# One mask product per bank and split value products for the last 64 queries of an attention kernel

## The chip, the core and the metric

The kernel runs on one core of one Trainium2 chip. Times are device microseconds of that core for one launch. Five engines run side by side, each through its own instructions in their order: TensorE (PE, with its weight loads listed apart as PEld), VectorE (DVE), ScalarE (ACT), GpSimd (POOL) and SyncE (SP, which issues most DMAs). TensorE writes its products to PSUM, eight banks of 512 float32 columns on 128 partitions.

## The reference

Three layers follow one another: attention, a mixture of experts, and a two-layer network.

```python
scores = (q @ k.transpose(0, 1, 3, 2)) / sqrt(D)      # q, k, v: B, H, S, D = 4, 8, 576, 64
scores = where(triu(ones(S, S), k=1), -1e9, scores)   # causal mask
a = exp(scores - scores.max(-1)); a /= a.sum(-1) + 1e-9
local = a @ v
q_p = where(q > 0, q, exp(q) - 1) + 1
mem_out = (q_p @ M_prev) / (q_p . z_prev + 1e-6)
attn = g * mem_out + (1 - g) * local                  # g = sigmoid(beta), per head
x = moe(attn as 2304 rows of 512)    # 8 experts, the best one for each row that is not skipped
out = leaky_relu(x @ w_in) @ w_out   # 512 -> 2048 -> 512
```

## The kernel before, in words

The 32 pairs of batch and head are worked in eight groups `n` of four heads. The 576 queries of a head lie in blocks of 128, 128, 128, 128 and 64 (`ROWS`). A slot (`slot`, L716) is one head and one half of its queries: half `hf` = 0 holds queries 0 to 255, half 1 queries 256 to 575. There are 32 slots of each half. In a slot

- `mm`/`mx` (L726, L733) make the scores with queries on partitions, and DVE takes each row's maximum; `q2t`/`q2e` (L753, L758) turn minus that maximum into two extra rows of the second operand;
- the second `mm` (L772 to L776) makes the scores again, with keys on partitions, in the banks that `BLK` lists. An entry (o, j, r0) is key block j against the queries from r0 on, written from column o. Half 0 has one bank, half 1 three. Each entry is a product L772 (128 x 128 weights, float32r), a product L774 that adds the low part and the maximum (66 rows), and, where the block touches the diagonal, a product L776 of the triangle `tri16` and `negi` (both bfloat16), which adds -1e30 above the diagonal;
- `exp` (L781, ACT) writes the exponentials of a bank to `pT`;
- `pv` (L802) multiplies them with the values and a column of ones, in float32, 64 queries at a time: 64 columns of `pT` are the weights, 65 columns of `vn` stream through, and the sums land on partitions 0 to 63 (m = 0) or 64 to 127 (m = 64) of a PSUM tile `pv`. Each float32 product is two weight loads and two matmuls in the trace. A query block of 128 has products on both halves of the partitions in turn; the last block, of 64 queries, has its five (one for each key block) all on partitions 0 to 63.

When both heads of a pair are done, `final` (L820) divides by the sums of the ones column (`f1` to `f3`: L834, L835, L839, L844), scales into `xb` (`f4`: L852, L854) and adds the memory part on POOL (`f5`: L862). The tile `pv` is one of two banks (`PVB` = 2), and it is free when `f4` is done. There are 32 finals, 16 of them of half 1, which hold the last query block.

The order on each engine is made by a list scheduler in the program (`Sched`): each task has an engine, a duration in ns, its predecessors, a key (its due time) and what it takes of the pools ("s": six score banks, "v": the two `pv` banks, and so on). In its simulated time the scheduler gives an idle engine the ready task of lowest key. The durations are constants in the code: for `pv` 181 for each key block of a full query block and 122 for each of the last one. Between these tasks the same engines also work on other things that the scheduler puts in: the copies that split q and k into high and low parts, 32 chunks of a weight conversion on ACT, DVE and POOL (L319 to L339), the routing of rows to experts, and at the end the first tiles of the first expert (`early`).

Of the kernel before, what the change touches and what calls it, by code (L numbers as in the profile page):

```python
# [10 lines left out]
F32 = mybir.dt.float32  # L11
# [6 lines left out]
AF = mybir.ActivationFunctionType  # L18
ALU = mybir.AluOpType
# [10 lines left out]
EK, WS = 39944.504, 485.0  # L30
PT0, PTX, PTH, PT2 = 0.3, -0.1, -0.17, -1427.4
MAN = {ET.PE, ET.Activation, ET.DVE, ET.Pool}
BLK = [[[(0, 0, 0), (256, 1, 128)]], [[(0, 0, 0), (320, 3, 128)], [(0, 1, 0), (320, 4, 256)], [(0, 2, 0)]]]
OFF = [[0], [0, 512, 896]]
SP = [[[(0, 0, 0, 128), (1, 128, 0, 256)]], [[(2, 0, 0, 384)], [(3, 0, 0, 512)], [(4, 0, 0, 256)], [(4, 0, 256, 320)]]]
EXPS = [[384], [512, 384, 320]]
# [94 lines left out]
class K:  # L131
# [579 lines left out]
    def slot(self, n, b, g, hf, h, T, d, get, put):  # L711
        nc, add, st = self.nc, self.sc.add, self.st
        O1, O2, O3, O4 = OFS[hf]
        q1, k1, k2, qb, vn, col = d["q1"], d["k1"], d["k2"], d["qb"], d["vn"], d["col"]
        xs = (0,) if hf == 0 else (0, 1, 2)
        ni, i0 = 2 + hf, 2 * hf  # L716
        u = {}
        kd = get(*[("k1", n, h, x) for x in xs], *[("q1", n, h, x) for x in xs[hf:]])
        ttr = []
        for p, parts in enumerate(SP[hf]):  # L720
            def mm(parts=parts, p=p):
                if p == 0:
                    u["m8"] = self.m8.pop(0)
                u["s", p] = s = self.T_tile()
                for i, o, c0, w in parts:
                    nc.tensor.matmul(s[:, o:o + w], col(1, h, 128 * i), k1[:, h, c0:c0 + w], start=True, stop=True)  # L726

            def mx(parts=parts, p=p):
                s = u.pop(("s", p))
                for i, o, c0, w in parts:  # L730
                    R = ROWS[i]
                    m = u["m8"][:R, i - i0:i - i0 + 1]
                    nc.vector.tensor_tensor_reduce(out=self.y[:R, 0:w], in0=s[:R, o:o + w], in1=self.mb[:R, max(0, MB[i] + c0):max(0, MB[i] + c0) + w],  # L733
                                                   scale=1.0, scalar=-3e38 if c0 == 0 else m, op0=ALU.add, op1=ALU.max, accum_out=m)
            pe = sum(max(w / 2.4 + 3, ROWS[i] / 1.2) for i, o, c0, w in parts)
            dv = sum(w / .96 + 73 + (60 if c0 else 0) for i, o, c0, w in parts)
            a = add("PE", pe, mm, kd + (get(("m8r", n)) if 0 else []), T + p, ["s"] + (["m8"] if p == 0 else []))
            put(("s", n), a)
            ttr.append(add("DVE", dv, mx, [a] + ttr[-1:], T + O1 * (p + 1) / len(SP[hf]), (), ["s"]))

        def sp():
            m8 = u["m8"]
            self.m8.append(m8)
            q = qb[:, i0:i0 + ni, h, 64:66]
            nc.vector.tensor_reduce(out=q[:, :, 0], in_=m8[:, 0:ni, None], axis=AX.X, op=ALU.max, negate=True)
            nc.vector.scalar_tensor_tensor(q[:, :, 1], m8[:, 0:ni], -1.0, q[:, :, 0].bitcast(F32), op0=ALU.mult, op1=ALU.subtract)
        put("ttr", *ttr)
        a = add("DVE", 145, sp, ttr, T + O1, (), ["m8"])

        def q2t():  # L750
            u["qt"] = t = self.T_tile(F32R)
            for x in range(ni):
                nc.tensor.transpose(t[:66, 128 * x:128 * x + 128], qb[:, i0 + x, h], self.idr)  # L753

        def q2e():
            w = 256 + 64 * hf
            u["q2"] = q2 = self.ap3.tile([128, 320], F32R, tag="q2", name="q2")
            nc.scalar.activation(q2[:66, :w], u.pop("qt")[:66, :w].bitcast(F32), AF.Copy)  # L758
        a = add("PE", (114, 175)[hf], q2t, [a] + get(*[("ql", n, x) for x in xs[hf:]]), T + O2, ["s"])
        for x in xs[hf:]:  # L760
            put(("q2t", n, x), a)
        a = add("ACT", (264, 318)[hf], q2e, [a], T + O2 + 1, ["q2"], ["s"])
        kd = get(*[("k2", n, h, x) for x in xs])
        ex = {}
        nb = len(BLK[hf])
        for p, (bank, o1, w) in enumerate(zip(BLK[hf], OFF[hf], EXPS[hf])):
            def mm(bank=bank, p=p):
                u["t", p] = t = self.T_tile()
                for o, j, r0 in bank:
                    q0, q1_ = 256 * hf + r0, (256, S)[hf]  # L770
                    R, w = ROWS[j], q1_ - q0
                    nc.tensor.matmul(t[:, o:o + w], col(0, h, 128 * j), q1[:, h, q0:q1_], start=True, stop=False)  # L772
                    diag = q0 == 128 * j
                    nc.tensor.matmul(t[:, o:o + w], col(2, h, 128 * j)[:66], u["q2"][:66, r0:r0 + w], start=False, stop=not diag)  # L774
                    if diag:
                        nc.tensor.matmul(t[:, o:o + R], self.tri16, self.negi[:, :R], start=False, stop=True)  # L776

            def exp(o1=o1, w=w, p=p):
                if p == 0:
                    u["pT"] = self.ap3.tile([128, (384, 1216)[hf]], F32, tag=f"pT{hf}", name="pT", bufs=2)  # L780
                nc.scalar.activation(u["pT"][:, o1:o1 + w], u.pop(("t", p))[:, 0:w], AF.Exp, scale=0.125)  # L781

            pe = sum(2 * max((256 + 64 * hf - r0) / 2.4 + 3, ROWS[j] / 1.2) + 60 * (256 * hf + r0 == 128 * j) for o, j, r0 in bank)
            m_ = add("PE", pe, mm, [a] + kd, T + O3 + p, ["s"])
            put(("st", n), m_)
            e_ = add("ACT", w / 1.2 + 51, exp, [m_] + list(ex.values())[-1:], T + O3 + p + .5,
                     [f"pT{hf}"] if p == 0 else [], ["s"] + (["q2"] if p == nb - 1 else []))
            for o, j, r0 in bank:
                ex[j] = e_
        pos = {j: OFF[hf][k] + o - r0 for k, bank in enumerate(BLK[hf]) for o, j, r0 in bank}  # L790
        r, hh = h // 2, h % 2
        pvs = []
        for x in range(ni):
            def pv(x=x):
                if hh == 0 and x == 0:
                    st["pv", n, hf, r] = self.psP.tile([128, 512], F32, tag="p", name="pv")
                t, i = st["pv", n, hf, r], i0 + x
                R, o = ROWS[i], 130 * x + 65 * hh
                for j in range(i + 1):
                    c = pos[j] + 128 * x  # L800
                    for m in range(0, R, 64):
                        nc.tensor.matmul(t[m:m + 64, o:o + 65], u["pT"][:, c + m:c + m + 64], vn[:, j, h], start=(j == 0), stop=(j == i))  # L802
            i = i0 + x
            first = hh == 0 and x == 0
            pvs.append(add("PE", sum(181 if ROWS[i] == 128 else 122 for j in range(i + 1)), pv,
                           [ex[j] for j in range(i + 1)] + pvs[-1:] + get(("lv", n)) + ([] if first else get(("pv0", n, hf, r))), T + O4 + x,
                           ["v"] if first else [], [f"pT{hf}"] if x == ni - 1 else []))
            if first:
                put(("pv0", n, hf, r), pvs[-1])
        put(("vuse", n), *pvs)  # L810
        if hf:
            put("pvs1", *pvs)
        put(("pv", n, hf, r), *pvs)
        if hh == 1:
            self.final(n, b, g, hf, r, T + O4 + FIN, d["ec"], get, put)

    def final(self, n, b, g, hf, r, T, ec, get, put):
        nc, add, st = self.nc, self.sc.add, self.st
        ni, i0 = 2 + hf, 2 * hf
        u = {}  # L820
        cuts = [(0, 2, 128), (2, 3, 64)][:1 + hf]

        def mem():
            u["s"] = s = self.T_tile()
            for x in range(ni):
                nc.tensor.matmul(s[:, 130 * x:130 * x + 130], ec(r, i0 + x), self.mm[b % 2][:, 2 * g + r], start=True, stop=True)

        def f1():
            u["n"] = self.nl.pop(0)
            pv = st.pop(("pv", n, hf, r))  # L830
            u["sv"] = u["s"][:, 0:130 * ni].rearrange("p (x c) -> p x c", x=ni)
            u["pv"] = pv[:, 0:130 * ni].rearrange("p (x h c) -> p x h c", x=ni, h=2)
            for x0, x1, R in cuts:
                nc.vector.tensor_scalar(u["n"][:R, x0:x1, 1], u["pv"][:R, x0:x1, :, D], 1e-9, None, op0=ALU.add)  # L834
            nc.vector.tensor_scalar(u["n"][:, 0:ni, 0], u["sv"][:, :, 128:130], 1e-6, None, op0=ALU.add)  # L835

        def f2():
# [8 lines left out]
        def f4():  # L846
# [2 lines left out]
                st["xb", b] = self.ap2.tile([128, NB, DM], F32, tag="xb", name="xb")  # L849
            u["m2"] = m2 = self.ap2.tile([128, 3, 2, D], F32, tag="m2", name="m2")  # L850
            for x0, x1, R in cuts:
                nc.vector.tensor_tensor(xv(x0, x1, R), u["pv"][:R, x0:x1, :, 0:D],  # L852
                                        rl[:R, x0:x1, 1, :, None].to_broadcast([R, x1 - x0, 2, D]), op=ALU.mult)
            nc.vector.tensor_tensor(m2[:, 0:ni], u["sv"][:, :, 0:128].rearrange("p x (h d) -> p x h d", h=2),  # L854
                                    rl[:, 0:ni, 0, :, None].to_broadcast([128, ni, 2, D]), op=ALU.mult)
# [6 lines left out]
            nc.gpsimd.tensor_tensor(xv(x0, x1, R), u["m2"][:R, x0:x1], xv(x0, x1, R), op=ALU.add)  # L862
        m = add("PE", 226 * ni, mem, get(("eT", n), ("mm", b)), T - MK, ["s"])
        put(("mem", n), m)
        a = add("DVE", 140 + 70 * hf, f1, [m] + get(("pv", n, hf, r)), T, ["nl"])
        a = add("DVE", (100, 135)[hf], f2, [a], T)
        a = add("DVE", 80, f3, [a] + get("gl"), T, (), ["nl"])
        war = get(("xbuse", b - 2))
# [810 lines left out]
```

## Time and profile before

| | us |
|---|---|
| three runs: lowest, median, highest | 886.28, 889.01, 889.37 |
| the profiled execution | 887.11 |
| its span from first to last instruction | 885.5 |
| TensorE busy in it (share) | 850.9 (96%) |
| VectorE, ScalarE, GpSimd busy (share) | 630.7 (71%), 480.8 (54%), 198.5 (22%) |

Some 1.6 us of the profiled execution lie outside its span. The attention fills the first 325 us or so, the experts run until 490 us, and the rest is the two-layer network. A busy share of TensorE counts matmuls that overlap in its pipeline, and their ends are modelled; how long a piece of its work takes is therefore read from the start of its first matmul to the start of the next piece.

### The profile page before, as it was taken

To read this page: it belongs to the slowest core of one execution; us is meant where nothing else is said; L and a number is where in the kernel's file an instruction comes from. 1 tells how busy PE (TensorE), PEld (TensorE's weight loads), DVE (VectorE), ACT (ScalarE), POOL (GpSimd) and SP (SyncE) were. 2 spreads that over 40 slices of the span, in tenths; PEclk is the share of its full clock that TensorE was granted. 3 is DMA by queue.
4 is the path that set the end of the run, shared out by engine and by line. 5 is a ranking of instruction groups with operands and counts; after the bars stand their busy time and mean duration, and the time that the engine had idled before them with its cause. 6 is when DMAs were issued, how large, how long until landed. Compare 5 with 4: busy or idle time off the path is not lost. (4 is left out here: it accounts for less than half of the span.)

```text
span 885.5 us, 19666 instructions
## 1 busy us (share of the span) xinstructions
PE 850.9 (96%) x7432; PEld 758.6 (86%) x7432; DVE 630.7 (71%) x1786; ACT 480.8 (54%) x921; POOL 198.5 (22%) x262
## 2 busy tenths in 40 slices
PE   6999999999999899998999999999999999999997
PEld 5887888887788777676667899999999999999997
DVE  6779787879878986578575589765656565656565
ACT  8897886877876562666554355433333333333332
POOL 5546444654532733222220000000000000000000
PEclk9699997999999999999999999999999999999999
DMA  6747765566357394899562401010101010101000
GB/s 147 191 130 187 200 198 141 124 152 199 75 193 274 123 336 127 298 341 344 176 244 89 171 1 48 1 49 1 48 1 49 1 48 2 48 2 48 1 24 24
DMA packets 103947, 107.61 MB, mean 122 GB/s; under 512 B 69661, under 2 KB 69789, under 8 KB 103828
## 3 DMA queue, kind: packets, MB, share of 16 engines
q1 hardware_dynamic: 101190, 100.90, 36.7%
q0 software_dynamic: 2640, 5.21, 2.0%
q8 instruction: 67, 1.10, 0.5%
q14 instruction: 50, 0.41, 0.2%
HBM read 81.57 MB, written 25.86 MB: 121 GB/s over the span
## 5 line engine op out<-in xcount | busy, mean ns | idle before, releaser
L1594 PE MATMUL g<-sw,ah 128*128 128x256 f32 x448 | 126.0, 281 | 0.0
L1593 PE MATMUL g<-sw,ah 128*128 128x256 f32 x448 | 125.7, 281 | 0.0
L1545 DVE SCALAR_TENSOR_TENSOR ua<-ua 128x512 f32<-128x512 f32 x72 | 49.6, 689 | 80.2 <-ACT ua L1494 80.2
L1494 ACT ACTIVATE ah<-ua 128x384 fp32r<-128x384 f32 (+1 forms) x72 | 38.8, 539 | 110.4 <-PE g L1595 78.4
L1494 ACT ACTIVATE ua<-t 128x512 f32<-128x512 f32 x72 | 43.0, 597 | 101.1 <-PE t L1538 101.1
L733 DVE CUSTOM_DVE_ANT_0 v<-t,v 128x512 f32<-128x512 f32 (+4 forms) x160 | 75.4, 471 | 27.9 <-PE t L726 22.3
L1595 PE MATMUL g<-sw,al 128*128 128x256 f32 x320 | 89.8, 281 | 0.0
L802 PE MATMUL pv<-vn,pT 128*64 128x65 f32 x1600 | 86.8, 234 | 2.5 <-DVE xb L852 2.0
L802 PEld LDWEIGHTS pv<-vn,pT 128*64 128x64 f32 x1600 | 68.4, 141 | 22.4 <-issue 13.3
L1593 PEld LDWEIGHTS g<-sw,ah 128*128 128x128 f32 x448 | 84.4, 188 | 0.0
L1594 PEld LDWEIGHTS g<-sw,ah 128*128 128x128 f32 x448 | 84.3, 188 | 0.0
L781 ACT ACTIVATE pT<-t 128x384 f32<-128x384 f32 (+2 forms) x128 | 62.2, 501 | 31.9 <-PE t L776 30.4
L1535 PE MATMUL t<-x,v 128*128 128x256 f32 x288 | 71.9, 283 | 0.7 <-ACT x L1416 0.7
L1536 PE MATMUL t<-x,a 128*128 128x256 f32 x288 | 71.0, 280 | 0.5 <-DVE a L1083 0.5
L1536 PE MATMUL t<-x,v 128*128 128x256 f32 x288 | 71.1, 279 | 0.0
L1535 PE MATMUL t<-x,a 128*128 128x256 f32 x288 | 71.0, 280 | 0.0
L1595 PEld LDWEIGHTS g<-sw,al 128*128 128x128 f32 x320 | 60.9, 190 | 0.0
L1535 PEld LDWEIGHTS t<-x,v 128*128 128x128 f32 x288 | 54.3, 188 | 1.2 <-ACT x L1416 0.9
L1536 PEld LDWEIGHTS t<-x,a 128*128 128x128 f32 x288 | 54.1, 188 | 0.7 <-DVE a L1083 0.7
L1536 PEld LDWEIGHTS t<-x,v 128*128 128x128 f32 x288 | 54.1, 188 | 0.3
L1535 PEld LDWEIGHTS t<-x,a 128*128 128x128 f32 x288 | 54.1, 188 | 0.0
L862 POOL TENSOR_TENSOR xb<-m,xb 128x256 f32<-128x256 f32 (+1 forms) x48 | 35.8, 758 | 79.9 <-DVE m L854 58.3
(365 smaller groups left out, 2341.9 us busy)
## 6 DMA issues: line engine op xcount, KB each, us to landing
c<-in_moe_w_dram SPq DMA_DIRECT2D x32, 512.0 KB, 6.3
va<-in_moe_w_dram SPq DMA_DIRECT2D x21, 512.0 KB, 8.5
v<-in_moe_w_in_dram SPq DMA_DIRECT2D x16, 512.0 KB, 4.7
v<-in_moe_w_out_dram SPq DMA_DIRECT2D x16, 512.0 KB, 5.2
xe<-x SPq DMA_DIRECT2D x18, 256.0 KB, 2.9
out_dram<-xe SPq DMA_DIRECT2D x18, 256.0 KB, 2.1
a<-in_k_dram SPq DMA_DIRECT2D x32, 128.0 KB, 2.9
a<-in_q_dram SPq DMA_DIRECT2D x32, 128.0 KB, 3.8
```

What stands on the lines that cost most here:

```text
L733: nc.vector.tensor_tensor_reduce(out=self.y[:R, 0:w], in0=s[:R, o:o + w], in1=self.mb[:R, max(0, MB[i] + c0):max(0, MB[i] + c0) + w], scal ...
L781: nc.scalar.activation(u["pT"][:, o1:o1 + w], u.pop(("t", p))[:, 0:w], AF.Exp, scale=0.125)
L802: nc.tensor.matmul(t[m:m + 64, o:o + 65], u["pT"][:, c + m:c + m + 64], vn[:, j, h], start=(j == 0), stop=(j == i))
L862: nc.gpsimd.tensor_tensor(xv(x0, x1, R), u["m2"][:R, x0:x1], xv(x0, x1, R), op=ALU.add)
L1494: tt_, cp = V.tensor_tensor, lambda o, i: A.activation(o, i, AF.Copy)
L1535: nc.tensor.matmul(o, wih[k][:, fs], xh[:, k], start=(k == 0), stop=False)
L1536: nc.tensor.matmul(o, wil[k][:, fs], xh[:, k], start=False, stop=False)
L1545: V.scalar_tensor_tensor(u, u, 0.01, u, op0=ALU.mult, op1=ALU.max)
L1593: nc.tensor.matmul(o, ah, wh, start=(p == z == 0), stop=False, skip_group_check=True)
L1594: nc.tensor.matmul(o, ah, wl, start=False, stop=False, skip_group_check=True)
L1595: nc.tensor.matmul(o, al, wh, start=False, stop=(p == 7), skip_group_check=True)
```

## The change

Three things are changed in the attention.

- `BLK` of half 1 is dealt anew: its first bank now holds the two full diagonal blocks (key block 3 from column 0 and key block 2 from column 192), and the third bank holds key block 0, which has no diagonal. The sizes of the banks stay.
- In a bank with two diagonal blocks, the two mask products become one, of 2 x 128 columns. The products of the second entry no longer begin an accumulation of their own (`start` is only set at column 0).
- The products of the last query block with the values go to partitions 0 to 63 for even key blocks and to partitions 64 to 127 for odd ones. In `final` of half 1 a new ACT task `fe` copies the upper half (64 x 130) to SBUF, a new first instruction of `f1` on DVE adds the lower half to it, and `f1` and `f4` take the last block from that sum. The scheduler's durations go from 122 to 75 for these products, `fe` has 170, and `f1` of half 1 has 100 more.

```diff
-BLK = [..., [[(0, 0, 0), (320, 3, 128)], [(0, 1, 0), (320, 4, 256)], [(0, 2, 0)]]]
+BLK = [..., [[(0, 3, 128), (192, 2, 0)], [(0, 1, 0), (320, 4, 256)], [(0, 0, 0)]]]
...
+                dg = []
                 for o, j, r0 in bank:
...
-                    nc.tensor.matmul(t[:, o:o + w], col(0, h, 128 * j), q1[:, h, q0:q1_], start=True, stop=False)
+                    nc.tensor.matmul(t[:, o:o + w], col(0, h, 128 * j), q1[:, h, q0:q1_], start=(o == 0), stop=False, skip_group_check=True)
...
                     if diag:
-                        nc.tensor.matmul(t[:, o:o + R], self.tri16, self.negi[:, :R], start=False, stop=True)
+                        dg.append((o, ROWS[j]))
+                if len(dg) == 2:
+                    z = dg[1][0]
+                    nc.tensor.matmul(t[:, 0:2 * z].rearrange("p (a b) -> p a b", a=2)[:, :, 0:128], self.tri16,
+                                     self.negi[:, None, :].to_broadcast([128, 2, 128]), start=False, stop=True, skip_group_check=True)
+                elif dg:
+                    (o, R), = dg
+                    nc.tensor.matmul(t[:, o:o + R], self.tri16, self.negi[:, :R], start=False, stop=True, skip_group_check=True)
...
                 for j in range(i + 1):
                     c = pos[j] + 128 * x
+                    if R == 64:
+                        m = 64 * (j % 2)
+                        nc.tensor.matmul(t[m:m + 64, o:o + 65], u["pT"][:, c:c + 64], vn[:, j, h], start=(j < 2), stop=(j > i - 2))
+                        continue
...
+        def fe():
+            u["e"] = e = self.ap2.tile([128, 1, 2, 65], F32, tag="ev", name="ev")
+            v = st["pv", n, hf, r][64:128, 260:390].rearrange("p (x h c) -> p x h c", x=1, h=2)
+            nc.scalar.activation(e[:64], v, AF.Copy)
...
+            if hf:
+                e = u["e"]
+                nc.vector.tensor_tensor(e[:64], u["pv"][:64, 2:3], e[:64], op=ALU.add)
+            u["part"] = lambda x0, x1, R: u["e"][:64] if R == 64 else u["pv"][:, x0:x1]
...
-        a = add("DVE", 140 + 70 * hf, f1, [m] + get(("pv", n, hf, r)), T, ["nl"])
+        z = [add("ACT", 170, fe, get(("pv", n, hf, r)), T)] if hf else []
+        a = add("DVE", 140 + 170 * hf, f1, [m] + z + get(("pv", n, hf, r)), T, ["nl"])
```

Over the whole attention the mask products go from 160 to 96. Since the durations change, the scheduler also deals the neighbouring work a little differently; on TensorE an instruction stands some five places from where it stood, and from the experts on the order is the same.

On TensorE, the first slot of half 1 (b: the keys, q: the extra rows, tri: the triangle, t: a score bank). Before, from the first bank's mask on:

```order
L776 LDWEIGHTS tri_139
L776 MATMUL t<-negi,tri_139 128x128
L772 MATMUL t<-b_86 128x320
L774 MATMUL t<-q_555,b_86 128x320
L772 MATMUL t<-b_86 128x64
L774 MATMUL t<-q_555,b_86 128x64
L776 LDWEIGHTS tri_139
L776 MATMUL t<-negi,tri_139 128x64
L772 MATMUL t<-b_86 128x320
L774 MATMUL t<-q_555,b_86 128x320
L776 LDWEIGHTS tri_139
L776 MATMUL t<-negi,tri_139 128x128
```

The same place now, from the second entry of the first bank on:

```order
L773 MATMUL t<-b_86 128x320
L775 MATMUL t<-q_551,b_86 128x320
L780 LDWEIGHTS tri_139
L780 MATMUL t<-negi,tri_139 128x2x128
L773 MATMUL t<-b_86 128x320
L775 MATMUL t<-q_551,b_86 128x320
L773 MATMUL t<-b_86 128x64
L775 MATMUL t<-q_551,b_86 128x64
L784 LDWEIGHTS tri_139
L784 MATMUL t<-negi,tri_139 128x64
L773 MATMUL t<-b_86 128x320
L775 MATMUL t<-q_551,b_86 128x320
```

The mask of the first bank covers both blocks, and the third bank ends without one.

On VectorE, the first final of half 1 (m: row maxima, nl and rl: the divisors, cg and v: a converted chunk). Before:

```order
L733 ISA v_85,m_98<-t,v_85,m_98 64x320
L733 ISA m_98 64x1
L333 TENSOR_SCALAR cg<-cg 128x512
L834 TENSOR_SCALAR nl_101<-pv 128x2x2
L834 TENSOR_SCALAR nl_101<-pv 64x2
L835 TENSOR_SCALAR nl_101<-t 128x3x2
L330 SCALAR_TENSOR_TENSOR v_85<-v_85 128x512
L839 RECIPROCAL rl<-nl_101 128x12
```

Now:

```order
L852 TENSOR_TENSOR ev<-pv,ev 64x130
L855 TENSOR_SCALAR nl_101<-pv 128x2x2
L855 TENSOR_SCALAR nl_101<-ev 64x2
L856 TENSOR_SCALAR nl_101<-t 128x3x2
L733 ISA v_85,m_98<-t,v_85,m_98 64x320
L733 ISA m_98 64x1
L333 TENSOR_SCALAR cg<-cg 128x512
L330 SCALAR_TENSOR_TENSOR v_85<-v_85 128x512
L860 RECIPROCAL rl<-nl_101 128x12
```

The sum of the two halves stands in front of the final, and the row maximum of the next slot comes behind the final's first part here.

On ScalarE, at the same final (q: the extra rows, pT: the exponentials, a and b: q and k parts). Before:

```order
L663 ACTIVATE b_86<-t 128x2x256
L627 ACTIVATE a_82<-a_82 128x512
L664 ACTIVATE b_86<-t 64x2x256
L781 ACTIVATE pT<-t 128x384
L670 ACTIVATE b_86<-t 128x2x256
L758 ACTIVATE q_987<-t 66x320
L627 ACTIVATE a_82<-a_82 128x512
```

Now:

```order
L663 ACTIVATE b_86<-t 128x2x256
L670 ACTIVATE b_86<-t 128x2x256
L664 ACTIVATE b_86<-t 64x2x256
L789 ACTIVATE pT<-t 128x384
L758 ACTIVATE q_972<-t 66x320
L843 ACTIVATE ev<-pv 64x130
L627 ACTIVATE a_82<-a_82 128x512 x2
```

The copy of the upper half stands in the queue between the copy of the extra rows and work of the next group.

## Rows read from the trace of the kernel before

**Rows 1.** The page: span, and busy us (share) of each engine.

```profile
span 885.5 us, 19666 instructions
PE 850.9 (96%) x7432; PEld 758.6 (86%) x7432; DVE 630.7 (71%) x1786; ACT 480.8 (54%) x921; POOL 198.5 (22%) x262
```

**Rows 2.** Stretches (us): length, engines' busy us (instructions), granted clock, DMA share, GB/s.

```profile
25.00:200.00 175.00, 170.61 (x1912) 146.33 (x1912) 139.61 (x512) 140.16 (x312) 87.65 (x106) 0.93 0.63 165
200.00:225.00 25.00, 22.95 (x277) 19.72 (x276) 23.21 (x92) 18.32 (x42) 11.08 (x13) 1.00 0.64 194
...
275.00:300.00 25.00, 23.72 (x279) 19.80 (x279) 22.51 (x98) 11.75 (x27) 9.10 (x11) 1.00 0.70 245
300.00:325.00 25.00, 23.67 (x272) 19.68 (x271) 22.17 (x57) 15.43 (x28) 14.61 (x12) 1.00 0.59 198
...
345.00:490.00 145.00, 133.50 (x626) 95.69 (x625) 92.56 (x110) 82.83 (x120) 33.62 (x25) 1.00 0.69 240
490.00:885.00 395.00, 390.13 (x3222) 385.57 (x3221) 257.26 (x650) 144.14 (x257) 0.97 (x1) 1.00 0.09 30
```

**Rows 3.** Timeline of PE, value products: start, us, operation, out<-in, shape, count.

```profile
289.57 0.80 PE L802 MATMUL pv<-vn,pT 128*64 128x65 f32 x10
290.30 0.82 PE L726 MATMUL t<-c 128*128 128x320 f32 x3
291.04 0.57 PE L802 MATMUL pv<-vn,pT 128*64 128x65 f32 x12
291.54 0.38 PE L753 MATMUL t<-idr,v 128*66 128x128 f32 x3
...
292.10 0.69 PE L802 MATMUL pv<-vn,pT 128*64 128x65 f32 x16
292.72 0.42 PE L772 MATMUL t<-c 128*128 128x320 f32 x1
```

**Rows 4.** Timeline of PE, the router's products on four column strips.

```profile
326.92 0.64 PE L914 MATMUL t<-xT,wgs 128*32 128x128 f32 x16
327.50 0.51 PE L521 MATMUL o<-v,eh 128*128 128x512 f32 x1
```

**Rows 5.** Timeline of PE, score products with and without a mask between.

```profile
154.49 0.28 PE L774 MATMUL t<-q,c 66*128 66x256 f32 x1
154.61 0.23 PE L776 MATMUL t<-negi,tri 128*128 128x128 bf16 x1
154.65 0.31 PE L772 MATMUL t<-c 128*128 128x128 f32 x1
154.79 0.27 PE L774 MATMUL t<-q,c 66*128 66x128 f32 x1
...
298.66 0.31 PE L774 MATMUL t<-q,c 66*128 66x320 f32 x1
298.81 0.25 PE L772 MATMUL t<-c 128*128 128x192 f32 x1
298.90 0.27 PE L774 MATMUL t<-q,c 66*128 66x192 f32 x1
```

**Rows 6.** Groups of one shape: count, busy us, mean ns, idle us before.

```profile
L852 DVE TENSOR_TENSOR xb<-pv,rl 64x128 f32<-64x128 f32 x16 | 4.3, 271 | 0.0
L693 ACT ACTIVATE c<-t 128x128 f32<-128x128 f32 x4 | 1.1, 284 | 0.0
```

**Rows 7.** Waits of PE up to 345 us: us in total, times, longest.

```profile
PE t L753 <- DVE v L746: 5.7, 7, 1.3
PE pv L802 <- DVE xb L852: 2.0, 3, 1.1
```

**Rows 8.** Timeline of DVE and PE at the end of a final of half 1.

```profile
193.41 0.60 DVE L852 TENSOR_TENSOR xb<-pv,rl 128x256 f32<-128x256 f32 x2
...
194.29 0.80 PE L802 MATMUL pv<-vn,pT 128*64 128x65 f32 x10
```

**Rows 9.** A stretch at the lower clock, columns as in group 2.

```profile
144.00:152.00 8.00, 8.00 (x62) 7.02 (x61) 4.27 (x19) 4.90 (x12) 2.88 (x5) 0.50 0.75 198
```

More of the change, by code (lines that the diff above doesn't have):

```diff
@@ L32 @@
 MAN = {ET.PE, ET.Activation, ET.DVE, ET.Pool}
-BLK = [[[(0, 0, 0), (256, 1, 128)]], [[(0, 0, 0), (320, 3, 128)], [(0, 1, 0), (320, 4, 256)], [(0, 2, 0)]]]
+BLK = [[[(0, 0, 0), (256, 1, 128)]], [[(0, 3, 128), (192, 2, 0)], [(0, 1, 0), (320, 4, 256)], [(0, 0, 0)]]]
 OFF = [[0], [0, 512, 896]]
@@ L768, in mm @@
                 u["t", p] = t = self.T_tile()
+                dg = []
                 for o, j, r0 in bank:
                     q0, q1_ = 256 * hf + r0, (256, S)[hf]
-                    R, w = ROWS[j], q1_ - q0
-                    nc.tensor.matmul(t[:, o:o + w], col(0, h, 128 * j), q1[:, h, q0:q1_], start=True, stop=False)
+                    w = q1_ - q0
+                    nc.tensor.matmul(t[:, o:o + w], col(0, h, 128 * j), q1[:, h, q0:q1_], start=(o == 0), stop=False, skip_group_check=True)
                     diag = q0 == 128 * j
-                    nc.tensor.matmul(t[:, o:o + w], col(2, h, 128 * j)[:66], u["q2"][:66, r0:r0 + w], start=False, stop=not diag)
+                    nc.tensor.matmul(t[:, o:o + w], col(2, h, 128 * j)[:66], u["q2"][:66, r0:r0 + w], start=False, stop=not diag, skip_group_check=True)
                     if diag:
-                        nc.tensor.matmul(t[:, o:o + R], self.tri16, self.negi[:, :R], start=False, stop=True)
+                        dg.append((o, ROWS[j]))
[6 more added lines that the diff above has]
+                    nc.tensor.matmul(t[:, o:o + R], self.tri16, self.negi[:, :R], start=False, stop=True, skip_group_check=True)
             def exp(o1=o1, w=w, p=p):
@@ L804, in slot @@
             first = hh == 0 and x == 0
-            pvs.append(add("PE", sum(181 if ROWS[i] == 128 else 122 for j in range(i + 1)), pv,
+            pvs.append(add("PE", sum(181 if ROWS[i] == 128 else 75 for j in range(i + 1)), pv,
                            [ex[j] for j in range(i + 1)] + pvs[-1:] + get(("lv", n)) + ([] if first else get(("pv0", n, hf, r))), T + O4 + x,
@@ L832, in f1 @@
             u["pv"] = pv[:, 0:130 * ni].rearrange("p (x h c) -> p x h c", x=ni, h=2)
+            if hf:
+                e = u["e"]
+                nc.vector.tensor_tensor(e[:64], u["pv"][:64, 2:3], e[:64], op=ALU.add)
+            u["part"] = lambda x0, x1, R: u["e"][:64] if R == 64 else u["pv"][:, x0:x1]
             for x0, x1, R in cuts:
-                nc.vector.tensor_scalar(u["n"][:R, x0:x1, 1], u["pv"][:R, x0:x1, :, D], 1e-9, None, op0=ALU.add)
+                nc.vector.tensor_scalar(u["n"][:R, x0:x1, 1], u["part"](x0, x1, R)[:, :, :, D], 1e-9, None, op0=ALU.add)
             nc.vector.tensor_scalar(u["n"][:, 0:ni, 0], u["sv"][:, :, 128:130], 1e-6, None, op0=ALU.add)
@@ L851, in f4 @@
             for x0, x1, R in cuts:
-                nc.vector.tensor_tensor(xv(x0, x1, R), u["pv"][:R, x0:x1, :, 0:D],
+                nc.vector.tensor_tensor(xv(x0, x1, R), u["part"](x0, x1, R)[:, :, :, 0:D],
                                         rl[:R, x0:x1, 1, :, None].to_broadcast([R, x1 - x0, 2, D]), op=ALU.mult)
```

## The prediction

> **What bounds the kernel now.** I read the busy shares first [rows 1]: TensorE works 96% of the span, VectorE 71%, and no other engine more than 54%. A mean over three layers says little, so the stretches come next [rows 2]. The change touches the attention, up to about 325 us. From 25 to 200 us TensorE is idle for 175 - 170.61 = 4.4 us (2.5%), while VectorE is 139.61/175 = 80% busy. From 200 to 225 us VectorE is at 93% and TensorE idles 2.05 us (8.2%); from 275 to 300 us the figures are 90% and 5.1%, from 300 to 325 us 89% and 5.3%. The reader is to see two things. TensorE is the bound nearly everywhere, so work taken from it should shorten the attention. And where VectorE comes near 90%, TensorE begins to wait: its longest waits among the repeated ones are for the row maxima (`t L753 <- DVE v L746`, 5.7 us in 7 places [rows 7]).
>
> What follows must not take the gain back. From 345 to 490 us TensorE is busy 133.50 of 145 us with DMA at 0.69, and from 490 us on 390.13 of 395 [rows 2]: neither stretch is held by a transfer that began at a fixed time, and the expert weights are requested after buffers of the last group fall free. So an attention that ends x us earlier should move the end by x.
>
> **What it removes.** The last query block: ten matmuls (five products of two), all on partitions 0 to 63, take 290.30 - 289.57 = 0.73 us up to the next piece [rows 3]. Twelve that change sides after every two take 291.54 - 291.04 = 0.50 us, and sixteen 292.72 - 292.10 = 0.62 us: 0.03 us for each further one. Ten in the new order (two low, two high, two low, two high, two low) should then take 0.50 - 0.06 = 0.44 us, and each of the 32 slots of half 1 saves 0.29 us: 9.3 us. What the trace does not show is this order with a new moving operand at each change of sides; in the twelve both sides take the same values. The nearest row that has it is the router: four column strips, each with its own weights and its own moving operand, 16 matmuls in 327.50 - 326.92 = 0.58 us, 0.036 us each although each streams 128 columns [rows 4]. So different operands do overlap. Bounds: nothing saved (no overlap) and 32 x (0.73 - 10 x 0.036) = 11.8 us. I take 9.3, since the twelve have the same shape and type.
>
> Twelve matmuls on changing sides in 0.50 us beside ten on one side in 0.73 us [rows 3] show that the two sides overlap for this shape. A rule says otherwise: by the Trainium skill (TensorE: Matmul & The Clock Gate, Part 3, "What overlaps and what doesn't") a weight load overlaps matmuls in flight only when the row group differs, and here both sides use all 128 rows; by it the ten would still take 0.73 us and this term would be zero. The trace does not agree with it for the twelve, and I follow the rows.
>
> Masks: 64 products fall away (one in each of the 64 slots), but their columns do not, since the merged product streams 256. What goes is one change of weights. From L774 to the next L774 with a mask between, 256 + 128 + 128 = 512 columns take 154.79 - 154.49 = 0.30 us; without one, 320 + 192 = 512 columns take 298.90 - 298.66 = 0.24 us [rows 5]. So one change costs 0.06 us, and 64 of them 3.8 us. Bounds: nothing, if the change of weights is hidden in either case, and 64 x (154.79 - 154.61 - 0.05) = 8.3 us, where a mask and the product behind it, 0.18 us, shrink to the 128 columns of the latter (0.05 us by the 512 columns in 0.24). I take the nearer pair of rows, 3.8 us.
>
> TensorE thus loses 9.3 + 3.8 = 13.1 us of work over some 300 us.
>
> **What it adds.** Sixteen copies of 64 x 130 on ScalarE; the nearest row is the copy of 128 x 128 from PSUM, 0.284 us [rows 6]: 4.5 us in all. Sixteen sums of 64 x 130 on VectorE; the nearest row is the product of 64 x 128 from PSUM, 0.271 us [rows 6]: 4.3 us. The later reads of the last block, now from SBUF, I leave at their price. Neither engine is the bound, so these lie beside TensorE's work, but the cover thins. From 25 to 200 us VectorE would hold 139.6 + 175/300 x 4.3 = 142.1 us in 175 - 175/300 x 13.1 = 167.4 us, 85% instead of 80%. From the four stretches, TensorE's idle share goes from 2.5% at 80% to 6.2% at 90.5% (the mean of the three others), 0.35 points for each point. Five points cost 1.8% of some 290 us: 5 us. Bounds: nothing (the new order keeps TensorE fed), and 10 us, twice that, since the order around the finals is dealt anew.
>
> The copy and the sum also stand in front of `f1`, and so lengthen the time until the `pv` bank is free. Behind the waiting sum on VectorE stand the row maxima of the next slot, behind the copy on ScalarE the exponentials. TensorE waits for a `pv` bank only 2.0 us in 3 places now [rows 7], so I put no separate price here; it is the first rival.
>
> The sum: -9.3 - 3.8 + 5 = -8.1 us on the profiled execution, 887.11 us with what lies around its span: 879 us. That execution is 1.9 us under the median of the runs (889.01) and within their spread, so I forecast 880 us, against a level of about 888.
>
> **The rivals.**
>
> *The value banks become the bound.* Each final of half 1 holds its `pv` bank longer by the copy, the sum and the copy's place in ScalarE's queue. In the final at 193.41 us the bank falls free at 194.01 and the next piece of value products starts at 194.29 [rows 8], 0.28 us of slack. The two new instructions take 0.284 + 0.271 = 0.55 us, and if each finds one mean instruction ahead of it in its queue (480.8/921 = 0.52 us on ScalarE, 630.7/1786 = 0.35 us on VectorE [rows 1]), 0.87 us more. Less the slack that is 1.14 us; if TensorE stood still for it at all 16 finals, 18 us would be lost against 13 saved: 5 us slower than the level of 888, or 893 us. The gain is gone from 13.1/16 = 0.82 us at each final, and the kernel is slower by more than 4.4 us from 1.1 us. Against it: two banks, other products to put in between, and only 2.0 us of such waits now. Chance 0.14, of which 0.10 ends slower.
>
> *The halves do not overlap.* Then the value products save nothing and the masks 3.8 us. VectorE's share goes to 142.1/(175 - 2.2) = 82%, 2.4 points more, which by 0.35 points each and 290 us costs 2.4 us: 888 - 1.4 = 887 us, no change that can be told. Rows 3 and 4 speak against it; that no row has just this order speaks for it. Chance 0.07.
>
> *The clock.* From 144 to 152 us TensorE ran at a granted clock of 0.50, the lower level of 1.2 GHz, though it was busy all 8 us [rows 9]. Such a stretch costs about half its length, 4 us. A new order can add one (880 + 4 = 884 us, no change that can be told) or remove one. Chance 0.12 that one or two are added, 0.02 of it slower.
>
> *TensorE stays fed.* No more waiting than now: 888 - 13 = 875 us. Chance 0.05.
>
> **How the numbers follow.** The forecast (gain of 4.5 to 12 us) has 0.62. What a measurement of this kernel can tell from no change is about 0.5%, 4.4 us. Faster by more: 0.62 + 0.05 = 0.67. Within: 0.07 + 0.10 + 0.04 = 0.21. Slower: 0.10 + 0.02 = 0.12. The range reaches down to the largest saving of both terms less some waiting, 872 us, and up to 889, which takes in the clock, the case without overlap and the mild end of the first rival; the far end of that rival, 0.1, is left out above, and some 0.06 below.
>
> **What the changed profile would show.** Right: the ten matmuls of the last block in about 0.44 us to the next piece; no mask product between the first bank's entries and two of them less in each head; TensorE's idle time up to 325 us grown by about 5 us, mostly on waits for VectorE; the first loads of the experts' second stage some 8 us earlier, and the same length from there to the end. Wrong: ten matmuls still in 0.7 us; waits `pv <- xb` or waits for `ev` that add up to 10 us; a stretch at the lower clock that was not there; or an end of the attention 8 us earlier that the experts do not pass on.

## The result and the profile after

Over all runs of the first comparison the changed kernel took 879.54 us (median; 875.68 to 882.67), the kernel before 889.14 us (886.28 to 889.37). The ratio is 0.9894, with a 95% interval from 0.986 to 0.9928. The same kernel run again, with the experiments, gave 882.37 us and 0.992 (0.9889 to 0.995). So the change is worth some 7 to 10 us. Times, ratios and means from here on leave out the seven runs, of some 230, that took over 1.5% longer than the fastest of their kernel.

The profiled execution took 882.67 us, the slowest of its four. The page, to be laid against [rows 1]:

```profile
span 881.0 us, 19572 instructions
PE 839.9 (95%) x7368; PEld 745.4 (85%) x7368; DVE 629.6 (71%) x1802; ACT 484.5 (55%) x937; POOL 195.7 (22%) x262
```

TensorE's work went from 850.9 to 839.9 us, 11.0 less; its idle time grew from 885.5 - 850.9 = 34.6 to 41.1 us, 6.5 more. In between lies the gain of this pair, 4.5 us. The repeat was profiled too:

```profile
span 877.4 us, 19572 instructions
PE 838.8 (96%) x7368; PEld 745.3 (85%) x7368; DVE 630.6 (72%) x1802; ACT 483.9 (55%) x937; POOL 195.9 (22%) x262
```

Here it is 12.1 us less work and 38.6 - 34.6 = 4.0 more idle, 8.1 us gained. The same kernel thus shows both, and the mean is taken from the runs, not from one profile.

The stretches of the profiled execution, as in [rows 2], and the part up to the first load of the experts' routing table and behind it:

```profile
25.00:200.00 175.00, 165.83 (x1878) 139.37 (x1878) 141.35 (x523) 141.84 (x320) 86.82 (x104) 0.93 0.63 168
200.00:225.00 25.00, 23.79 (x298) 19.70 (x292) 21.99 (x93) 19.47 (x47) 13.06 (x16) 1.00 0.66 197
275.00:300.00 25.00, 22.90 (x254) 18.78 (x250) 22.15 (x96) 14.28 (x30) 11.33 (x13) 1.00 0.60 227
300.00:325.00 25.00, 21.70 (x262) 16.95 (x261) 22.97 (x57) 15.76 (x28) 8.61 (x12) 1.00 0.75 267
0.00:343.10 343.10, 318.75 (x3534) 265.56 (x3535) 280.02 (x1044) 257.71 (x562) 164.51 (x240) 0.97 0.62 179
343.10:881.00 537.90, 521.18 (x3836) 479.85 (x3834) 349.55 (x759) 226.80 (x375) 31.21 (x22) 1.00 0.25 86
```

The same cut before, at the same load:

```profile
0.00:349.60 349.60, 331.90 (x3609) 281.03 (x3610) 282.04 (x1029) 254.52 (x546) 167.34 (x240) 0.97 0.61 176
349.60:885.50 535.90, 519.03 (x3824) 477.54 (x3823) 348.65 (x757) 226.25 (x375) 31.18 (x22) 1.00 0.25 86
```

The load comes 6.5 us earlier (9.5 in the repeat). Up to it TensorE is idle 343.10 - 318.75 = 24.35 us instead of 17.70, and most of the growth lies from 25 to 200 us, where it idles 9.2 us (before 4.4). Behind the load there are 12 matmuls more and 2.15 us more work: the new order moved them past this mark. The granted clock up to the load is 0.97 in both.

TensorE, the value products of the last block and a bank of half 0 with its one mask:

```profile
209.20 0.56 PE L811 MATMUL pv<-vn,pT 128*64 128x65 f32 x10
209.69 0.94 PE L838 MATMUL t<-mm,b 128*128 128x130 f32 x6
...
226.28 0.39 PE L773 MATMUL t<-c 128*128 128x256 f32 x1
226.51 0.29 PE L775 MATMUL t<-q,c 66*128 66x256 f32 x1
226.63 0.22 PE L773 MATMUL t<-c 128*128 128x128 f32 x1
226.69 0.27 PE L775 MATMUL t<-q,c 66*128 66x128 f32 x1
226.81 0.29 PE L780 MATMUL t<-negi,tri 128*128 128x256 bf16 x1
226.85 0.39 PE L726 MATMUL t<-c 128*128 128x320 f32 x1
```

The ten matmuls take 0.49 us to the next piece instead of 0.73 [rows 3]. They are six on the lower half (three even key blocks) and four on the upper (two odd ones), and the longer side sets the time: six on each side took 0.50 us before, eight on each 0.62 us, ten on one 0.73 us [rows 3], some 0.06 us for each one more on the longer side. The bank of half 0 takes 226.85 - 226.28 = 0.57 us; before it took 0.68:

```profile
153.46 0.39 PE L772 MATMUL t<-c 128*128 128x256 f32 x1
...
154.14 0.39 PE L726 MATMUL t<-c 128*128 128x320 f32 x1
```

Over 25 such places each the medians are 0.66 and 0.56 us. The three banks of half 1 together went only from 1.64 to 1.62 us.

The waits of TensorE up to 345 us, as in [rows 7]:

```profile
PE t L642 <- DVE a L597: 5.3, 1, 5.3
PE t L753 <- DVE v L746: 3.6, 6, 1.1
PE t L753 <- DVE v L745: 1.9, 2, 1.3
PE t L726 <- DVE m L875: 1.8, 2, 1.2
PE t L753 <- DVE m L733: 1.7, 2, 1.4
PE t L645 <- DVE m L733: 1.6, 1, 1.6
PE pv L814 <- DVE xb L873: 1.3, 1, 1.3
```

These, the longest, are all waits for VectorE, and the one for a value bank (`pv <- xb`) is 1.3 us, less than the 2.0 before. Over the whole list the waits for VectorE went from 15.9 to 19.6 us, those for ScalarE from 1.1 to 2.7. The finals, by shape (busy us, mean ns):

```profile
L873 DVE TENSOR_TENSOR xb<-ev,rl 64x128 f32<-64x128 f32 x16 | 6.0, 376 | 0.0
L855 DVE TENSOR_SCALAR nl<-ev 64x2 f32<-64x2 f32 x16 | 5.2, 323 | 0.0
L852 DVE TENSOR_TENSOR ev<-pv,ev 64x130 f32<-64x130 f32 x16 | 4.5, 279 | 0.0
L843 ACT ACTIVATE ev<-pv 64x130 f32<-64x130 f32 x16 | 4.5, 278 | 2.2 <-PE pv L811 1.8
```

Copy and sum have their prices. The two reads of the last block, now from SBUF, are dearer by their means: 376 ns where [rows 6] has 271, and 323 ns where the kernel before has

```profile
L834 DVE TENSOR_SCALAR nl<-pv 64x2 f32<-64x2 f32 x16 | 2.2, 140 | 0.0
```

The means hide two cases. Of the 16 short reads 12 take 160 to 163 ns, and of the 16 products 13 take 273 to 279 ns. The other seven stand beside an instruction of GpSimd and end just behind it. One of each kind:

```profile
62.13 0.16 DVE L855 TENSOR_SCALAR nl<-ev 64x2 f32<-64x2 f32 x1
...
95.14 1.31 POOL L336 TENSOR_TENSOR cg<-cg,v 128x512 int32<-128x512 int32 x1 [3.91 <-issue]
95.24 1.23 DVE L855 TENSOR_SCALAR nl<-ev 64x2 f32<-64x2 f32 x1
```

Before, with the block read from PSUM, such a neighbour did no harm: five of the 16 products stood beside one and took 269 to 273 ns, among them the second of this pair.

```profile
175.21 1.43 POOL L336 TENSOR_TENSOR cg<-cg,v 128x512 int32<-128x512 int32 x1 [3.83 <-DVE rl L844]
175.41 0.60 DVE L852 TENSOR_TENSOR xb<-pv,rl 128x256 f32<-128x256 f32 x2
```

This is not special to the new reads. In the thirteen traces 619 VectorE instructions take over 200 ns more than the median of their kind, and each of them ends only after a GpSimd instruction that ran beside it, by no more than about its usual duration. So part of VectorE's busy time is such standing still: 35.0 us before, 33.1 and 34.7 us in the two profiles of the change (all that instructions take above that median, where it is over 60 ns). Of TensorE's 6.9 us of waits for the extra rows before (`v`, L745 and L746), 4.5 us lie behind an L746 of over 0.7 us stretched in this way.

### The profile page after: what moved, and what is told of

Read it like the earlier page. It is cut to its first block, busy times and chain, and to the rows that moved or that the text cites. A ratio compares the mean times of both kernels' runs of the same rounds, so it can differ in the third digit from the quotient of the medians.

```text
span 881.0 us, 19572 instructions
## 1 busy us (share of the span) xinstructions
PE 839.9 (95%) x7368; PEld 745.4 (85%) x7368; DVE 629.6 (71%) x1802; ACT 484.5 (55%) x937; POOL 195.7 (22%) x262
## 5 line engine op out<-in xcount | busy, mean ns | idle before, releaser
L814 PE MATMUL pv<-vn,pT 128*64 128x65 f32 x1280 | 64.0, 236 | 1.8 <-DVE xb L873 1.3
L814 PEld LDWEIGHTS pv<-vn,pT 128*64 128x64 f32 x1280 | 48.7, 142 | 18.2 <-issue 12.3
L336 POOL TENSOR_TENSOR cg<-cg,v 128x512 int32<-128x512 int32 x32 | 42.1, 1316 | 55.3 <-issue 17.5
```

The lines of the kernel that those rows point to most:

```text
L336: nc.gpsimd.tensor_tensor(u["g"], u["g"], u["s"], op=ALU.add)
```

## The experiments

The change does two pieces of work, masks and split, and it also gives the scheduler new durations, which deal a new order. The theory tested was that of the prediction (the two pieces pay, the order only spreads the waits); the rivals were that one piece alone pays, or that the order does. The kernels below combine work and order.

| order | neither piece | masks alone | split alone | both |
|---|---|---|---|---|
| of before | 1 (889.4 us) | 0.9959 (0.9935 to 0.9983) | 1.0066 (1.0037 to 1.0095) | 1.0018 (0.9986 to 1.005) |
| of after | 0.9974 (0.9949 to 0.9999) | 0.9941 (0.9906 to 0.9975) | 0.9971 (0.9946 to 0.9995) | 0.992 (0.9889 to 0.995); first comparison 0.9894 |

Each ratio is to the kernel before in the same call, with its 95% interval. In the traces the kernels of one row run the same sequence of instructions on VectorE, ScalarE and GpSimd, but for the copy, the sum and their names; so a row holds the order and a column the work.

**Masks alone, order of before.** `BLK` and the second `mm` of the change; the scheduler sees the old columns (excerpt, against the kernel before).

```diff
-BLK = [..., [[(0, 0, 0), (320, 3, 128)], [(0, 1, 0), (320, 4, 256)], [(0, 2, 0)]]]
+BLK = [..., [[(0, 3, 128), (192, 2, 0)], [(0, 1, 0), (320, 4, 256)], [(0, 0, 0)]]]
+BLKP = (the old BLK, for the planned duration of mm alone)
```

> The kernel before with the mask change alone (new banks of half 1, one mask product for two diagonal blocks), and the scheduler given the durations of before, so that the work stands in the order of before. Theory 1, the saving is in the work removed: 64 changes of weights at 0.06 us, 3.8 us, of which TensorE's waits give some back: 2 to 4 us faster than before (ratio 0.996 to 0.998). Theory 2, the saving is in the new order of the work: no change (within 1 us). Theory 3, a mask's weights load hidden behind the product ahead: no change, and the trace shows the first bank of half 1 taking as long as before plus the 53 ns of 128 more columns.

Measured: 886.37 us, 0.9959: 3.6 us faster. The masks are worth their price by themselves.

**Split alone, order of before.** Excerpt, against the changed kernel.

```diff
-BLK, mm of the change
+BLK, mm of before
-sum(181 if ROWS[i] == 128 else 75 ...)     # pv
+sum(181 if ROWS[i] == 128 else 122 ...)
-add("ACT", 170, fe, ...)
+add("ACT", 0, fe, ..., lat=0)
-add("DVE", 140 + 170 * hf, f1, ...)
+add("DVE", 140 + 70 * hf, f1, ...)
```

> The kernel before with the split of the last block's value products alone (with the copy and the sum), in the order of before; the scheduler plans the copy at no time. Theory 1: 32 x 0.29 = 9.3 us less work on TensorE, less some 3 us of new waits: 5 to 8 us faster (ratio 0.991 to 0.994). Theory 2 (the new order does it): no change, or slower by the copy's waits. If the value banks were the bound: slower, since here nothing was moved into the gap that the copy opens.

Measured: 894.96 us, 1.0066: slower by 5.9 us, where theory 1 had 5 to 8 us faster. In this order the split loses, though its ten matmuls take less time.

**Both, order of before.** The changed kernel with the durations of the block above and the old columns for `mm`.

> Both changes in the order of before. Theory 1: about as fast as the changed kernel, 7 to 11 us under before (ratio 0.988 to 0.992), and near the sum of the two single changes. Theory 2: no faster than before by more than 2 us.

Measured: 891.01 us, 1.0018: the whole change, in the old order, gains nothing, where theory 1 had 7 to 11 us. Its profile shows where the time stands (its lines are one further down than in the changed kernel):

```profile
PEclk9797997999799999999999999999999999999999
```

The same row of the changed kernel (mean granted clock in 40 slices, tenths):

```profile
PEclk9899998899999999999999999999999999999999
```

Two of the falls, with TensorE's row in front of each; the columns are those of [rows 2] and [rows 3], with the idle time before and its releaser in brackets:

```profile
66.55 0.34 PE L815 MATMUL pv<-vn,pT 128*64 128x65 f32 x4 [0.70 <-DVE xb L874]
...
228.18 0.47 PE L754 MATMUL t<-idr,v 128*66 128x128 f32 x3 [1.61 <-DVE v L747]
```

```profile
66.00:68.00 2.00, 1.45 (x19) 1.26 (x21) 1.97 (x6) 1.76 (x5) 0.77 (x1) 0.95 0.95 214
68.00:78.00 10.00, 10.00 (x67) 8.69 (x66) 7.18 (x28) 5.98 (x15) 4.98 (x7) 0.50 0.85 237
226.00:228.00 2.00, 0.57 (x8) 0.39 (x4) 1.97 (x6) 1.47 (x3) 1.97 (x2) 1.00 0.96 254
228.00:238.00 10.00, 9.82 (x61) 8.84 (x63) 6.02 (x26) 5.69 (x14) 4.14 (x6) 0.51 0.57 150
```

The reader is to see the same thing twice: VectorE is busy 1.97 of 2 us, TensorE waits for it (0.70 us for a value bank, 1.61 us for the row maximum's rows), and the next 10 us run at 1.2 GHz, with TensorE busy for 10.00 and 9.82 us of them. In front of the second fall, most of VectorE's busy time is not work. The instruction that TensorE waits for takes 1.38 us beside one of GpSimd; in the same kernel it takes 0.17 us without such a neighbour:

```profile
115.86 0.17 DVE L747 SCALAR_TENSOR_TENSOR v<-m,v 128x3 fp32r<-128x3 f32 x1
...
226.66 1.38 DVE L747 SCALAR_TENSOR_TENSOR v<-m,v 128x3 fp32r<-128x3 f32 x1
226.70 1.30 POOL L337 TENSOR_TENSOR cg<-cg,v 128x512 int32<-128x512 int32 x1
```

The waits of this kernel are longer too:

```profile
PE t L754 <- DVE v L747: 7.7, 9, 1.6
PE pv L815 <- DVE xb L874: 2.8, 3, 1.4
```

**No change in work, order of after.** The kernel before, with the scheduler told 75 for `pv`, an empty task in place of the copy, a longer `f1` and the new columns (excerpt, against the kernel before).

```diff
-sum(181 if ROWS[i] == 128 else 122 ...)
+sum(181 if ROWS[i] == 128 else 75 ...)
+z = [add("ACT", 170, lambda: None, ...)] if hf else []
-add("DVE", 140 + 70 * hf, f1, [m] + ...)
+add("DVE", 140 + 170 * hf, f1, [m] + z + ...)
```

> The work of the kernel before, neither change in it, but the scheduler given the durations of the changed kernel (and an empty task in place of the copy), so that the work stands in the order of the changed kernel. Theory 1: within 3 us of before, and rather slower, since the order leaves room that nothing uses (ratio 0.998 to 1.005). Theory 2: 6 to 10 us faster, as fast as the changed kernel.

Measured: 887.28 us, 0.9974. Dealing the same work in the new order is worth 2.3 us, at the edge of what these runs can tell, and between the two expectations.

**Masks alone and split alone, order of after.** The block above with the masks; and the changed kernel with the old `BLK` and `mm`.

> The mask change alone, in the order of the changed kernel (an empty task in place of the copy). Work removed counts the same in any order: 3 to 4 us under the kernel with neither change in this order, which was at 0.9974: ratio 0.993 to 0.995. If only the pair of order and split counts: 0.997.

> The split alone, in the order of the changed kernel. In the order of before it made the kernel slower (1.0066), with 61 us of TensorE at 1.2 GHz against 24 in the trace of before. If the planned place of the copy is what decides: 5 to 8 us faster than before (ratio 0.991 to 0.994), with some 25 us at 1.2 GHz. If the split itself brings the lower clock, whatever the order: 1.000 or more, with 50 us or more at 1.2 GHz.

Measured: 882.98 us (0.9941) and 887.13 us (0.9971). In this order too the masks add their 3 us; the split alone adds nothing that the runs tell (0.9971 beside 0.9974), and neither of its expectations is met.

**Evens first.** The key blocks of the last query block in the order 0, 2, 4, 1, 3: one change of sides instead of four.

```diff
-for j in range(i + 1):
+for j in (range(i + 1) if R > 64 else (0, 2, 4, 1, 3)):
```

> The changed kernel with the five key blocks of the last query block taken as 0, 2, 4 and then 1, 3: the same products, copies and order of the work, but one change of sides instead of four. Theory 1, the saving comes from products on both sides running at once: the ten matmuls take some 0.65 us up to the next piece instead of 0.49, and of the 32 slots some 5 us are lost: 4 to 6 us slower than the changed kernel (ratio to before 0.994 to 0.997). Theory 2, the saving is in the order of the work alone: as fast as the changed kernel (0.989).

Measured: 882.15 us, 0.993 (0.9907 to 0.9954), not told from the changed kernel beside it (0.992). TensorE:

```profile
205.71 0.62 PE L811 MATMUL pv<-vn,pT 128*64 128x65 f32 x10
206.26 0.94 PE L838 MATMUL t<-mm,b 128*128 128x130 f32 x6
```

0.55 us, not far from 0.49: a miss of the expectation. One change of sides already brings most of the overlap, 0.18 of 0.24 us. What is lost, 32 x 0.06 = 1.9 us, is less than these runs tell, so the time does not decide between the two expectations; 0.55 us against 0.73 shows that the two sides do run at once.

**Copy and sum twice.**

```diff
             nc.scalar.activation(e[:64], v, AF.Copy)
+            nc.scalar.activation(e[:64], v, AF.Copy)
...
+                nc.vector.tensor_tensor(self.y[:64, 0:130]..., u["pv"][:64, 2:3], e[:64], op=ALU.add)
                 nc.vector.tensor_tensor(e[:64], u["pv"][:64, 2:3], e[:64], op=ALU.add)
```

> The changed kernel with the copy of the upper half done twice and the sum of the halves done twice (once into a scratch tile): 16 more ACT and 16 more DVE instructions of about 0.28 us, in the same order. If the copy and the sum are hidden beside TensorE: within 2 us of the changed kernel (ratio to before 0.988 to 0.992). If each holds a value bank that TensorE waits for: 16 x 0.55 = 9 us slower, no faster than before, with waits on xb that add up to 9 us. If short waits of TensorE are followed by stretches at 1.2 GHz, as the four runs ahead suggest: 2 to 6 us slower, more of it in the clock than in waits.

Measured: 887.1 us, 0.998 (0.9954 to 1.0006), against 882.37 us and 0.992 for the changed kernel: some 5 us for 16 more copies and 16 more sums, which are 16 x (0.278 + 0.279) = 8.9 us of engine time. They lie beside TensorE's work only in part. TensorE's waits, of the kinds shown above:

```profile
PE t L753 <- DVE v L746: 4.9, 6, 1.4
PE t L753 <- DVE v L745: 2.3, 2, 1.3
...
PE pv L814 <- DVE xb L875: 0.9, 1, 0.9
```

The wait for a value bank did not grow although the bank is held longer; the waits for what VectorE makes of the row maxima did (3.6 to 4.9 and 1.9 to 2.3 us, in one profile each). The banks are not what costs here.

**Half of the new plan.** Excerpts, against the changed kernel. Both pieces of work, with the scheduler told only of copy and sum (old 122 and old columns), or only of the shorter products (copy at 0, old `f1`).

```diff
-sum(181 if ROWS[i] == 128 else 75 ...)
+sum(181 if ROWS[i] == 128 else 122 ...)     # and the old columns for mm: the first kernel
```

```diff
-add("ACT", 170, fe, ...)
+add("ACT", 0, fe, ..., lat=0)
-add("DVE", 140 + 170 * hf, f1, ...)
+add("DVE", 140 + 70 * hf, f1, ...)          # the second kernel
```

> Both changes, with a plan that knows the time of the copy and of the sum, but still has the last block's value products at 122 ns a key block and the banks' times of before. If it is the planned place of the copy that keeps TensorE fed: as fast as the changed kernel (ratio 0.987 to 0.993), with about 25 us at 1.2 GHz. If it is the shorter products in the plan: as with the plan of before (1.0018). If any order near these gives what it gives by chance: anywhere between.

> Both changes, with a plan that knows the shorter value products (75) and the new banks, but plans the copy at no time and the sum not at all. If the planned place of the copy decides: no faster than before (ratio 0.998 to 1.005), with 45 us or more at 1.2 GHz. If the shorter products in the plan decide: 0.987 to 0.993.

Measured: 891.68 us (1.0035, 1.0008 to 1.0061) and 887.70 us (0.9969, 0.9936 to 1.0002). Told only of copy and sum, the scheduler deals an order no better than the old one (1.0018); told only of the shorter products, one that keeps less than half of the gain, which neither expectation had. The same work takes 882.37, 887.70, 891.68 and 891.01 us in four orders.

## Two costs in one time: work and clock

The orders differ in how long TensorE ran at its lower level, and each run lists its mean granted clock c. The lower level, 1.2 GHz, is half of 2.4, so a run of t us spent about 2 (1 - c) t us there. Over 220 runs of the twelve kernels (the first comparison, the calls of the experiments), a fit with a constant for each kernel and one slope for all gives 0.31 (0.28 to 0.35) us of time for each us at the lower level. With it the means part into a time at full clock and the clock's share. That is an estimate, since waits and falls come together; the bounds are 95%.

| kernel | mean us | us at 1.2 GHz | at full clock, against before |
|---|---|---|---|
| before | 889.4 | 20.0 | 0 |
| masks, old order | 886.5 | 21.6 | -3.4 ± 1.2 |
| split, old order | 896.1 | 45.0 | -1.2 ± 1.5 |
| both, old order | 892.0 | 44.5 | -5.1 ± 1.5 |
| neither, new order | 887.1 | 24.6 | -3.7 ± 1.2 |
| masks, new order | 883.2 | 22.1 | -6.9 ± 1.4 |
| split, new order | 887.0 | 30.6 | -5.8 ± 1.3 |
| both, new order (the change) | 881.0 | 24.3 | -9.8 ± 1.1 |
| the change, evens first | 882.7 | 24.3 | -8.1 ± 1.2 |
| the change, copy and sum twice | 887.4 | 31.7 | -5.7 ± 1.2 |
| both, planned with copy and sum only | 891.7 | 37.5 | -3.2 ± 1.3 |
| both, planned with the products only | 886.0 | 31.9 | -7.2 ± 1.3 |

By this estimate the pieces add up at full clock: the masks 3.4 us in the old order and 6.9 - 3.7 = 3.2 in the new; the split 1.2 or 5.1 - 3.4 = 1.7 in the old, 5.8 - 3.7 = 2.1 or 9.8 - 6.9 = 2.9 in the new; the order 3.7. Each has a bound of over 1 us, so the split's own gain is hardly told from nothing. The split brings time at the lower level with it, 45.0 - 20.0 = 25 us in the old order, which by the slope is 7.8 us and turns its gain into a loss; in the new order the change has 4 us more than before, 1.3 us of time.

The profiles show that the work removed does not hang on the order. If half of each trace's time at 1.2 GHz is taken off TensorE's busy time, a rough estimate of its work at full clock, the old work comes to 838.0 us in the old order and 837.3 in the new, the masks alone to 833.6 and 833.5, the split alone to 828.2 in either, both to 825.6 and 826.9. What the order changes is the waits and the clock.

## Why the prediction was right, and where it was not

The forecast of 880 us met the 879.5 of the first comparison, and the main steps stood: the work goes, and part of it comes back as waits for VectorE. That the number fits so closely is in part luck: the split brought less than its terms said, and the new order, which had no gain in the sum, made up for it.

- *Value products, 9.3 us: too large.* Ten matmuls take 0.49 us, not 0.44, so 32 slots save 32 x 0.24 = 7.7 us of TensorE. The halves do overlap, each with its own moving operand, but five key blocks do not split evenly. The prediction counted 0.03 us for each product on either side; the time goes by the longer side, which has six, as in the twelve that took 0.50 us. So [rows 3] had the figure: 32 x 0.23 = 7.4 us. The rule that was weighed (the Trainium skill, TensorE: Matmul & The Clock Gate, Part 3, "What overlaps and what doesn't"), by which the ten would stay at 0.73 us, is not what the trace shows for two column halves, nor with one change of sides (0.55).
- *Masks, 3.8 us: right in sum.* By the rows 32 x 0.10 + 32 x 0.02 = 3.8 us; by the runs 3.2 to 3.4 us. But it comes nearly all from half 0; why the merged mask of half 1, of as many columns, gains so little is not settled. (The upper bound of 8.3 us took 0.05 us for 128 of the 512 columns in 0.24 us; it is 0.06, and the bound 7.7 us.)
- *Work in all, 13.1 us:* 11.0 and 12.1 us less by the two profiles.
- *Waits, 5 us more: right in size,* 6.5 and 4.0 us by the two profiles, mostly on VectorE as said (3.7 of the 6.2 us of waits that the first profile has more up to the load), none on the banks. The reason given does not hold: VectorE's share was to rise by five points, and up to the load it rose by one (282.04 of 349.60 us, 280.02 of 343.10). That the size fits is luck; a busy share also counts the time in which VectorE stands beside GpSimd. The split costs what it hides behind: a second copy and sum cost 4.1 us at full clock, and 7 us more are spent at the lower level. So of its 7.7 us it keeps 1 to 3.
- *"The later reads of the last block, now from SBUF, I leave at their price": wrong in sum.* They take 105 and 183 ns more by their means, 16 x 0.288 = 4.6 us on VectorE, as much as the sum itself. Reading SBUF alone costs little (160 for 140 ns, 274 for 271); seven of the 32 reads last until a GpSimd instruction ends, and they make up over nine tenths of the 4.6 us.
- *The order, only as a cost: wrong.* Told the new durations, the scheduler deals the old work 2.3 us faster (3.7 at full clock). Without it the change would have been worth nothing (1.0018). This term, not in the sum, replaces what the split did not give.
- *The experts pass the shift on: right.* Behind the load stand 2.0 us more (1.4 in the repeat), for 12 matmuls that were moved past it, so the mark's 6.5 us are the span's 4.5.

The rivals. *Value banks:* not the bound; 1.3 us of waits for them now, 2.0 before, and 0.9 with the banks held longest. *No overlap:* fallen with the 0.49 us. *Clock:* small here (1.3 us), but it is what makes the old order lose; it deserved its chance, and a cause: both falls shown come behind a wait of TensorE for VectorE, and the kernel before has the same at 143 us, a wait of 1.10 us behind an L746 of 1.50 us beside GpSimd and then the stretch of [rows 9].

Open stays why just this order is the better one. One trait is shown: for equal work VectorE is busy less in it, in one profile each (before 630.7 us, 627.6 with the new order; masks 631.2 and 625.8; split 636.3 and 628.2; both 636.7 and 629.6). Half or more of each difference is time lost beside GpSimd: 35.0 and 33.4 us, 35.5 and 32.4, 36.7 and 30.9, 37.2 and 33.1. No run moves GpSimd's work alone, so none tells whether that is the cause. That TensorE waits less in the new order is not shown: with the old work it idles 34.6 us in the old and 37.6 us in the new, with 12.8 us less at the lower level.

## What to carry to other kernels

Where a scheduler deals the work from planned durations, test a change in two kernels: the new work in the old order, and the old work in the new order; here they gave 1.0018 and 0.9974, and both together 0.99. Work taken off the bounding engine counts only less the waits that its replacement makes on the engine that feeds it. Where work is dealt to two sides, price the longer side. Look behind a mean at the single instructions, and behind a busy share at what stands beside it: here three reads of over 0.5 us made 160 ns a mean of 323. Compare orders with the time at the lower clock beside the total.

## What the runs showed of the hardware

- Ten float32 matmuls (128 x 64 weights, 65 columns) take 0.73 us on one column half, 0.55 us with one change of halves, 0.49 us with four. Six and four on the halves take as long as six and six (0.50 us).
- In a kernel whose TensorE is busy 95%, waits of only 0.70 and 1.61 us preceded falls of the clock, each followed by 10 us at a granted clock of 0.50 or 0.51. By the fit a us at the lower level cost 0.31 us of time, not the half that was taken for it.
- Some VectorE instructions stand still beside GpSimd: all 619 that took over 200 ns more than the median of their kind ended only after a GpSimd instruction beside them. An addition of 64 x 2 from SBUF took 1.23 us instead of 0.16 so; two products from PSUM beside a GpSimd instruction of 1.43 us kept to 0.60 us.
